# Interleaved key and query transposes, and a planner term for small TensorE jobs, in an attention and two-MoE kernel

## The chip, the cores and the metric

One core of a Trainium2 chip runs the whole kernel in one launch. The metric is the device time of an execution in microseconds; a lower one is better.

## The reference, cut to what matters

Three parts follow each other: chunked attention with memory keys, a dense feed-forward layer, and a top-1 mixture of eight experts. The change touches the first alone.

```python
def _attn_ref(q, k, v, mem_k, mem_v):      # q, k, v: 4 x 8 heads x 768 x 64; 8 memory keys
    chunk, left_ctx, right_ctx = (32, 16, 8)
    ...
    for c in range(nc):
        ...
        k_full = np.concatenate([mem_k, k_ctx], axis=2)
        scores = scale * np.matmul(q_c, k_full.transpose(0, 1, 3, 2))
        a = np.exp(scores - np.max(scores, axis=-1, keepdims=True))
        a = a / (np.sum(a, axis=-1, keepdims=True) + 1e-09)
        out[:, :, c_start:c_end] = np.matmul(a, v_full)

def reference(**kwargs):
    ...
    x = _moe_ref(x=x, **moe_kwargs)         # h = x @ w_in; (h * tanh(softplus(h))) @ w_out
    return _moe2_ref(x=x, **moe2_kwargs)    # one expert of eight for each token
```

## The kernel before, in words

Attention goes by 48 blocks of 64 queries, all eight heads of a block at once. Blocks 0 to 17 are made by `blocks`, 18 to 47 by `chunks`; the diff changes `chunks` alone. An even block brings 96 new keys (8 of memory, 24 of context, 64 others) and the odd block behind it 64 more; the pair shares one tile of transposed keys, `kT`. For each block there are these jobs: load of queries and keys (`load_qk`, lines 545 to 557), the transposes `T` (lines 581 to 592: four of queries, line 586, and four of keys, line 588, each of two heads), copies `qT` and `kT` out of PSUM, the scores `S` (line 616, 32 small matmuls in parts of the array), maximum, exponential and normalisation on VectorE and ScalarE, the transposes `PT` of the probabilities (line 646), the values `V` (line 662, 32 small matmuls in parts), and their split into a high and a low part, which feed the dense layer.

The dense layer works in steps `H` (line 748, twelve matmuls of 384 columns) and `Y` (line 794, nine of 512). Its output tiles are transposed (`yT`, line 854) and multiplied with the expert embedding (`yL`, line 886). After all that come the routing tables and the experts, 13 units beside those that a device-side branch adds.

In the trace a TensorE instruction's shape stands before its operands: 64*128 is 64 rows of the array by 128 columns. A transpose multiplies a 64x128 piece of queries, as weights, with a 64x64 identity; a piece of an even block's keys has 96 rows and a 96x96 identity.

The order of all work on all engines is made when the program is built, by `Plan.order` (lines 136 to 195). It keeps a clock for each engine; each job has a time on each engine that can do it, a rank, the jobs it comes after, and the buffers that it gets and uses. Of the jobs that are ready within 34 ns of an engine's next free moment it takes the one with the lowest key (line 166), and for TensorE the first part of that key is whether the last job was "tiled" (`V`, and `S` without a mask) and this one isn't. `between` (lines 98 to 106) adds a fixed time where TensorE goes from dense to small jobs and back. Three PSUM buffers with the tag `a` serve the small jobs: `T` of a block gets two, `V` in `chunks` two, `S`, `PT`, `yT` and `yL` one each. The chip then runs each engine's jobs in that order, each waiting for what it needs.

Of the kernel before, what the change touches and what calls it, by code (L numbers as in the profile page):

```python
# [9 lines left out]
F32 = mybir.dt.float32  # L10
# [9 lines left out]
B, H, S, D = 4, 8, 768, 64  # L20
NMEM = 8
CHUNK, LEFT, RIGHT = 32, 16, 8
QB = 64
CTX = QB + LEFT + RIGHT
NK = CTX + NMEM
# [66 lines left out]
TICK, WARM = 10240 / 3, 3600  # L92
SHARE = dict(T=0.62, S=0.76)
LATENCY, START, SLACK = 2000.0, 1100.0, 34.0
DENSE = {"mm_h", "mm_y", "H", "Y"}


def between(a, b):

    if a in DENSE:  # L100
        return 92 if b in ("T", "S", "yL") else 0
    if b in DENSE:
        return 0 if a is None else 20 if a in ("PT", "yT", "xT", "hT") else 90
    return 93 if a in ("PT", "yT") and b in ("T", "S") else 0
# [6 lines left out]
class Plan:  # L111
# [5 lines left out]
    def job(self, key, fn, on, rank, after=(), get=(), use=(), lat=130, tiled=False):  # L117
        uses = list(use) + [h for _, h in get]
        for h in uses:
            self.users.setdefault(h, []).append(key)  # L120
        for _, h in get:
            self.getter[h] = key
        self.jobs[key] = dict(fn=fn, on=on, rank=rank, after=list(after), get=list(get), use=list(use), lat=lat, tiled=tiled,
                              need=[(tag, sum(t == tag for t, _ in get)) for tag in dict(get)])
# [11 lines left out]
    def order(self):  # L136
        end, on, free, todo, waits, tiled, last, cols, port = {}, {}, {}, {}, {}, False, None, {}, 0.0
        shared = lambda k, e: e == "Pool" and k[0] not in ("gather", "scatter", "issue", "experts") or e == "DVE" and k[0] in PORT
        held = {tag: [None] * n for tag, n in self.bufs.items()}
        for k, j in self.jobs.items():  # L140
            j["deps"] = set(j["after"]) | {self.getter[h] for h in j["use"] if self.getter[h] != k}
            todo[k] = len(j["deps"])
            for d in j["deps"]:
                waits.setdefault(d, []).append(k)
        self.log = []
        ready = {k: START for k, n in todo.items() if n == 0}
        while ready:
            cand = {}
            for k, r in ready.items():
                j = self.jobs[k]  # L150
                for tag, n in j["need"]:
                    rel = sorted(self.release(h, end) for h in held[tag])
                    r = max(r, rel[n - 1])
                if r < np.inf:
                    begin = lambda e: max(r, free.get(e, 0.0), port if shared(k, e) else 0.0)
                    t, e, d = min((begin(e) + d + (d if shared(k, e) else 0), e, d) for e, d in j["on"].items())
                    t = begin(e)

                    cand.setdefault(e, []).append((t, r if e == "Q" else j["rank"], k, d))
            if not cand:  # L160
                raise RuntimeError(f"no room for any of {list(ready)}")
            picks = []
            for e, c in cand.items():
                t = max(min(x[0] for x in c), free.get(e, 0.0))

                picks.append((e, *min((x for x in c if x[0] <= t + SLACK), key=lambda x: (e == "PE" and tiled > self.jobs[x[2]]["tiled"], x[1], x[0]))))
            e, t, rank, k, d = min(picks, key=lambda x: (x[1], x[0]))
            j = self.jobs[k]
            del ready[k]
            for tag, h in j["get"]:  # L170
                x = min(held[tag], key=lambda h: self.release(h, end))
                held[tag][held[tag].index(x)] = h
            if e == "PE":

                t0 = free.get(e, FILL0)
                while ("mm_h", 0) not in end and t0 + FILL < t:
                    self.log.append((t0, t0, e, None))
                    t0 = self.stream(cols, t0, FILL, 1)
                t = max(t, t0)
                t += between(last, k[0])  # L180
                last, tiled = k[0], j["tiled"]
                d = self.stream(cols, t, d, SHARE.get(k[0], 1)) - t
            free[e] = t + d
            if shared(k, e):
                port = t + d
            end[k] = t + d + j["lat"]
            on[k] = e
            self.log.append((t, t + d, e, k))
            for w in waits.get(k, ()):
                todo[w] -= 1  # L190
                if todo[w] == 0:
                    chain = "PE" in self.jobs[w]["on"]
                    ready[w] = max(end[x] - (130 if chain and on[x] == "PE" else 0) for x in self.jobs[w]["deps"])
        assert len(end) == len(self.jobs)
        return [(k, e) for _, _, e, k in self.log]
# [20 lines left out]
def attn_moe_moe_kernel(ctx, tc, q, k, v, mem_k, mem_v, w_in, w_out, emb, tau, w1, w2, cst, out, ydbg=None):  # L216
    nc = tc.nc
# [5 lines left out]
    ident = cf[:, 0:128]  # L223
# [10 lines left out]
    att = pa.enter_context(tc.tile_pool(name="att", bufs=1))  # L234
# [8 lines left out]
    def psa(shape, name):  # L243
        return ps_a.tile(shape, F32, tag="a", name=name)
# [3 lines left out]
    job, A, V_, G, E = plan.job, "Activation", "DVE", "Pool", "PE"  # L248
    engs = {A: nc.scalar, V_: nc.vector, G: nc.gpsimd}
    xt, yp = {}, {}  # L250
    tl = {}
# [278 lines left out]
    def chunks(u):  # L530
        b, i = divmod(u, NQB)
        j, o = divmod(u, SPB)
        R = lambda x: x + (1.4 * u - 17.5 if u < (LEAVE + 1) * SPB else 2 * o + 32 if j == LEAVE + 1 else 8 * u / 3 - 20.4)
        J = H // 2
        odd, pair = u % 2, u // 2
        w = QB * i - LEFT
        edge = 0 if i == 0 else 1 if i == NQB - 1 else None
        new = QB if odd else NMEM + PREV + QB
# [4 lines left out]

        def load_qk(e):
            qn = tl["qn", u] = att.tile([QB, H, D], F32, tag="qn", bufs=1, name="qn")
            kn = tl["kn", u] = att.tile([NK, H, D], F32, tag="kn", bufs=1, name="kn")
            get = lambda n, x, lo, hi: nc.sync.dma_start(out=kn[n:n + hi - lo], in_=x[b, :, lo:hi, :].rearrange("h p d -> p h d"))
            nc.sync.dma_start(out=qn, in_=q[b, :, i * QB:(i + 1) * QB, :].rearrange("h p d -> p h d"))
            if not odd:
                get(0, mem_k, 0, NMEM)  # L550
            lo, hi = w + (PREV if odd else 0), w + PREV + QB
            n = 0 if odd else NMEM
            if lo < 0:
                get(n, k, 0, -lo)
            if hi > NQB * QB:
                get(n + NQB * QB - lo, k, 0, hi - NQB * QB)
            get(n + max(-lo, 0), k, max(lo, 0), min(hi, NQB * QB))
# [23 lines left out]
        def T(e):  # L581
            p1 = psa([128, J, QB], "p_qT")
            p2 = psa([128, J, new], "p_kT")
            a, c = tl["qn", u], tl["kn", u]
            for n in range(J):
                nc.tensor.transpose(p1[:, n, :], a[:, 2 * n:2 * n + 2, :].rearrange("p h d -> p (h d)"), ident[:QB, :QB])
            for n in range(J):
                nc.tensor.transpose(p2[:, n, :], c[0:new, 2 * n:2 * n + 2, :].rearrange("p h d -> p (h d)"), ident[:new, :new])
            tl["T", u] = p1, p2
            tl["qT", u] = att.tile([128, J, QB], F32, tag="qT", name="qT")  # L590
            if not odd:
                tl["kT", pair] = att.tile([128, J, 5 * GR - NMEM], F32, tag="kT", name="kT")
# [78 lines left out]
        def x_lo(e):  # L671
            for a in range(2):
# [7 lines left out]
        t1, t2 = ("a", u, 1), ("a", u, 2)  # L680
        pss, pr, mxh, sm = ("pS", u), ("pr", u), ("mx", u), ("sm", u)
        kt, xb = ("kT", pair), [("X", u), ("X2", u)]
        job(("T", u), T, {E: 560 if odd else 630}, rank=R(0), after=[("qk", u)], use=[(t, u) for t in ("qn", "kn")] + ([kt] if odd else []),
            get=[("a", t1), ("a", t2), ("qT", ("qT", u))] + ([] if odd else [("kT", kt)]))
        job(("qT", u), qT, {A: 264, V_: 330}, rank=R(1), after=[("T", u)], use=[t1, ("qT", u)])
        job(("kT", u), kT, {A: 264, V_: 330} if odd else {A: 371 + 210, V_: 465 + 200}, rank=R(1), after=[("T", u)], use=[t2, kt])
# [22 lines left out]
             + [(j, f) for j in reversed(range(LEAVE)) for f in range(HALF, KFF)]  # L709
             + [(j, f) for j in range(LEAVE + 1, NBLK) for f in range(KFF)])  # L710
    at = {x: s for s, x in enumerate(order)}
    done = [TPB * j + t for j in sorted(range(NBLK), key=lambda j: at[j, KFF - 1]) for t in range(TPB)]
    y_p = dram.tile([LEAVE * BLK, DM], F32, name="y_p")
# [885 lines left out]
    for u in range(NSUB):  # L1599
        (blocks if u < BY_CHUNK else chunks)(u)  # L1600
# [7 lines left out]
    for kind, n in TURNS:  # L1608
        c = FIRST + 2 * n
# [50 lines left out]
```

## Time and profile before

| | us |
|---|---|
| median of three runs | 1073.29 |
| lowest, highest | 1073.01, 1078.38 |
| the profiled execution | 1077.64 |
| its span, first to last instruction | 1075.9 |
| TensorE busy | 1044.6 (97%) |
| VectorE busy | 751.5 (70%) |
| ScalarE busy | 692.2 (64%) |
| GpSimd busy | 168.0 (16%) |

The profiled execution is one of its own, not one of the three runs. Busy time of TensorE counts overlapping matmuls once; each matmul's record is longer than its share of the engine, since the next begins before it has ended. So the time that a group of matmuls takes is read from starts, not from durations.

### The profile page before, as it was taken

Reading aid. Unit: us, or ns where it says so; the run is one execution under the profiler, and the core shown is the slowest. Engines: PE = TensorE matmul, PEld = TensorE weight load, DVE = VectorE, ACT = ScalarE, POOL = GpSimd, SP = SyncE. Lnnn points to the kernel's source line nnn. Section 1 sums busy time; section 2 is a strip of 40 time slices with the busy share of each in tenths; the row PEclk is TensorE's granted clock in tenths of the full one; section 3 lists DMA queues with packets and bytes.
Section 4 is the critical chain, followed back from the end, with each engine's and each line's share of the span. In section 5 each row is a group of like instructions: output and inputs, shape, how many; then the busy total and the mean of one; then the engine's idle time right before and its main releaser. Section 6 shows DMA issues by size and latency. Waiting matters only on the chain. (4 is left out here: it accounts for less than half of the span.)

```text
span 1075.9 us, 22578 instructions
## 1 busy us (share of the span) xinstructions
PE 1044.6 (97%) x8404; PEld 912.3 (85%) x8404; DVE 751.5 (70%) x1607; ACT 692.2 (64%) x1617; POOL 168.0 (16%) x109
## 2 busy tenths in 40 slices
PE   8899999999999999999999999998999999999996
PEld 6678888998888888888888889888899888988995
DVE  5999996556756566556556556886978657777851
ACT  4888887777757777777777777855633444443441
POOL 0000100000000000000000000010135645655552
PEclk9899999999999999999999999998999999999998
DMA  7966540032331112112112100019459877568200
GB/s 192 258 195 183 160 128 23 1 101 62 97 80 40 41 41 60 40 43 61 41 40 70 28 17 31 1 27 378 173 188 399 292 227 250 170 216 268 88 30 22
DMA packets 164019, 128.09 MB, mean 119 GB/s; under 512 B 106229, under 2 KB 135285, under 8 KB 163647
## 3 DMA queue, kind: packets, MB, share of 16 engines
q1 hardware_dynamic: 159439, 111.63, 34.4%
q0 software_dynamic: 4464, 14.95, 3.9%
q8 instruction: 69, 1.13, 0.4%
q14 instruction: 47, 0.39, 0.1%
HBM read 119.19 MB, written 16.52 MB: 126 GB/s over the span
## 5 line engine op out<-in xcount | busy, mean ns | idle before, releaser
L748 PE MATMUL p_h<-xt,win_h 128*128 128x384 f32 x1024 | 273.3, 348 | 1.7 <-DVE rn L777 1.5
L748 PEld LDWEIGHTS p_h<-xt,win_h 128*128 128x128 f32 x1024 | 183.0, 190 | 9.4 <-DVE rn L777 3.2
L748 PE MATMUL p_h<-xt,win_l 128*128 128x384 f32 x512 | 174.2, 340 | 0.0
L767 DVE SCALAR_TENSOR_TENSOR m<-sq,rn 128x384 f32<-128x384 f32 x128 | 71.8, 561 | 123.1 <-ACT rn L256 122.4
L794 PE MATMUL p_y<-wout_h,gh 128*128 128x512 f32 x384 | 155.9, 406 | 0.5 <-DVE gh L266 0.5
L266 ACT CAST ehi<-eraw 128x1024 fp32r<-128x1024 f32 x89 | 92.8, 1048 | 98.5 <-PE p_y L1496 51.5
L1378 DVE TENSOR_TENSOR elo<-eraw,ehi 128x1024 fp32r<-128x1024 f32 x89 | 125.6, 1419 | 42.6 <-ACT ehi L266 35.8
L794 PE MATMUL p_y<-wout_h,gl 128*128 128x512 f32 x384 | 151.8, 395 | 0.0
L794 PE MATMUL p_y<-wout_l,gh 128*128 128x512 f32 x384 | 151.4, 394 | 0.0
L1496 PE MATMUL p_y<-ehi,hh 128*128 128x512 f32 x432 | 142.1, 398 | 1.0 <-DVE hh L1465 1.0
L1406 PE MATMUL p_h<-xs,ehi 128*128 128x256 f32 x704 | 129.5, 285 | 0.0
L752 ACT ACTIVATE sq<-p_h 128x384 f32<-128x384 f32 x128 | 62.4, 488 | 78.4 <-PE p_h L748 78.0
L1406 PEld LDWEIGHTS p_h<-xs,ehi 128*128 128x128 f32 x704 | 111.0, 191 | 1.6 <-DVE xs L1359 0.4
L1378 POOL TENSOR_TENSOR elo<-eraw,ehi 128x1024 fp32r<-128x1024 f32 x39 | 96.9, 2484 | 79.8 <-ACT ehi L266 51.7
L1406 PE MATMUL p_h<-xs,elo 128*128 128x256 f32 x352 | 100.4, 285 | 0.0
L771 ACT ACTIVATE m<-m,few 128x384 f32<-128x384 f32 x128 | 79.1, 618 | 32.1 <-DVE m L767 31.2
L1300 POOL DMA_INDIRECT vn<-y_d,gi x27 | 27.6, 1023 | 453.3 <-DVE si L1247 402.7
L1496 PEld LDWEIGHTS p_y<-ehi,hh 128*128 128x128 f32 x432 | 81.1, 188 | 19.6 <-DVE hh L1465 2.3
L748 PEld LDWEIGHTS p_h<-xt,win_l 128*128 128x128 f32 x512 | 97.0, 190 | 0.0
L794 PEld LDWEIGHTS p_y<-wout_h,gl 128*128 128x128 f32 x384 | 72.2, 188 | 17.7 <-DVE gl L785 0.4
L1496 PE MATMUL p_y<-elo,hh 128*128 128x512 f32 x216 | 85.3, 395 | 0.0
L774 DVE SCALAR_TENSOR_TENSOR rn<-m,rn 128x384 f32<-128x384 f32 x128 | 70.8, 553 | 20.4 <-ACT m L771 19.1
(285 smaller groups left out, 1872.3 us busy)
## 6 DMA issues: line engine op xcount, KB each, us to landing
eraw<-in_moe_w_dram SPq DMA_DIRECT2D x128, 512.0 KB
raw<-in_moe_w_in_dram SPq DMA_DIRECT2D x16, 512.0 KB
raw<-in_moe_w_out_dram SPq DMA_DIRECT2D x16, 512.0 KB
y_d<-ysb SPq DMA_DIRECT2D x24, 256.0 KB
qn<-in_q_dram SPq DMA_DIRECT2D x43, 128.0 KB
vn<-in_v_dram SPq DMA_DIRECT2D x114, 32.0 KB
vn<-in_v_dram SPq DMA_DIRECT2D x122, 24.0 KB
kn<-in_k_dram SPq DMA_DIRECT2D x22, 128.0 KB
```

The costliest lines, as they stand in the source:

```text
L266: (nc.scalar.copy if e == A else nc.vector.tensor_copy)(out, src)
L748: nc.tensor.matmul(p, w, xt[j][:, a, kk, :], start=(n == 0), stop=(n == len(ops) - 1))
L752: nc.scalar.activation(t, tl["h", s], AF.Tanh, scale=0.5)
L767: nc.vector.scalar_tensor_tensor(t, tl["sq", s], 4.0, tl["rn", s], ALU.add, ALU.mult)
L771: nc.scalar.activation(t, t, AF.Square, bias=c15)
L774: nc.vector.scalar_tensor_tensor(tl["rn", s], tl["m", s], 0.75, tl["rn", s], ALU.add, ALU.mult)
L794: nc.tensor.matmul(yp[yh][t], x[:, c], w[g][:, o, :], start=(first and n == 0), stop=(final and n == 2))
L1300: nc.gpsimd.indirect_dma_start(out=tl["xg", u, a], out_offset=None, in_=y_d[0:T1 * 128, :] if g == 1 else y_d[:, :], in_offset=bass.Indire ...
L1378: engs[e].tensor_sub(tl["elo", j], raw[b, second, c], tl["ehi", j].bitcast(F32))
L1406: nc.tensor.matmul(p[:, o, :], w[:, kk, s], v[:, kk, :], start=(kk == 0 and m == 0), stop=(kk == KDM - 1 and m == 2))
L1496: nc.tensor.matmul(tl["yy", u][a], v[:, kk, s], w[:, k, :], start=(kk == 0 and m == 0), stop=(kk == KEF - 1 and m == 2))
```

## The change

Three things. In `chunks`, the key tile becomes 128 partitions tall, and an odd block's 64 new keys are loaded to its partitions 64 to 127, where they were on 0 to 63; an even block's 96 stay on 0 to 95. The transposes of queries and of keys, which were two loops of four, become one loop that issues one of each in turn, for odd and even blocks alike; the odd keys' use the lower right part of the identity. And the planner gets a time of 330 for an odd block's `T` in place of 560, and a new reason to put a job late on TensorE: the last job was one of `T`, `S`, `V`, `yL`, and this one isn't.

```diff
+SMALL = {"T", "S", "V", "yL"}
...
-                picks.append((e, *min((x for x in c if x[0] <= t + SLACK), key=lambda x: (e == "PE" and tiled > self.jobs[x[2]]["tiled"], x[1], x[0]))))
+                picks.append((e, *min((x for x in c if x[0] <= t + SLACK), key=lambda x: (e == "PE" and (tiled > self.jobs[x[2]]["tiled"] or last in SMALL and x[2][0] not in SMALL), x[1], x[0]))))
...
-            kn = tl["kn", u] = att.tile([NK, H, D], F32, tag="kn", bufs=1, name="kn")
+            kn = tl["kn", u] = att.tile([128, H, D], F32, tag="kn", bufs=1, name="kn")
...
-            n = 0 if odd else NMEM
+            n = QB if odd else NMEM
...
             a, c = tl["qn", u], tl["kn", u]
+
+            r = slice(QB, QB + new) if odd else slice(0, new)
             for n in range(J):
                 nc.tensor.transpose(p1[:, n, :], a[:, 2 * n:2 * n + 2, :].rearrange("p h d -> p (h d)"), ident[:QB, :QB])
-            for n in range(J):
-                nc.tensor.transpose(p2[:, n, :], c[0:new, 2 * n:2 * n + 2, :].rearrange("p h d -> p (h d)"), ident[:new, :new])
+                nc.tensor.transpose(p2[:, n, :], c[r, 2 * n:2 * n + 2, :].rearrange("p h d -> p (h d)"), ident[r, r])
...
-        job(("T", u), T, {E: 560 if odd else 630}, rank=R(0), after=[("qk", u)], use=[(t, u) for t in ("qn", "kn")] + ([kt] if odd else []),
+        job(("T", u), T, {E: 330 if odd else 630}, rank=R(0), after=[("qk", u)], use=[(t, u) for t in ("qn", "kn")] + ([kt] if odd else []),
```

## Rows read from the trace of the kernel before

**Rows 1.** The page: busy time of each engine, and TensorE's granted clock in 40 slices.
```profile
PE 1044.6 (97%) x8404; PEld 912.3 (85%) x8404; DVE 751.5 (70%) x1607; ACT 692.2 (64%) x1617; POOL 168.0 (16%) x109
...
PEclk9899999999999999999999999998999999999998
```

**Rows 2.** TensorE's waits, those for the keys' copies: us in total, times, longest us.
```profile
PE p_S L616 <- ACT kT L266: 3.8, 2, 2.1
```

**Rows 3.** Windows: stretch, length, busy us (instructions) by engine; then granted clock, DMA share, GB/s.
```profile
150.00:158.00 8.00, 6.43 (x37) 5.37 (x35) 8.00 (x17) 7.61 (x18) 0.00 (x0) 1.00 0.44 117
...
230.00:620.00 390.00, 388.49 (x3805) 333.84 (x3804) 244.80 (x593) 288.80 (x794) 0.60 (x1) 1.00 0.22 54
320.50:324.00 3.50, 3.25 (x55) 2.29 (x52) 2.90 (x6) 3.18 (x8) 0.00 (x0) 1.00 0.54 170
```

**Rows 4.** Groups of TensorE by form: count, busy us, mean ns of one, idle before.
```profile
L586 PE MATMUL p_qT<-cf,qn 64*128 64x64 f32 x120 | 13.9, 237 | 0.0
...
L588 PE MATMUL p_kT<-cf,kn 96*128 96x96 f32 x60 | 8.2, 260 | 0.0
L588 PE MATMUL p_kT<-cf,kn 64*128 64x64 f32 x60 | 6.3, 228 | 0.0
...
L886 PE MATMUL p_lg<-embT,yb 128*128 128x24 bf16 x84 | 5.5, 176 | 0.0
```

**Rows 5.** Timeline of TensorE, an odd block's transposes: start, length of the run, count.
```profile
301.24 0.46 PE L586 MATMUL p_qT<-cf,qn 64*128 64x64 f32 x4
301.53 0.41 PE L588 MATMUL p_kT<-cf,kn 64*128 64x64 f32 x4
301.87 0.62 PE L748 MATMUL p_h<-xt,win_h 128*128 128x384 f32 x2
```

**Rows 6.** Timeline of TensorE, values and scores, the same columns.
```profile
304.18 0.67 PE L662 MATMUL p_X<-pT,vn 64*64 64x32 f32 x32
304.78 0.65 PE L616 MATMUL p_S<-kT,qT 64*32 64x64 f32 x32
```

**Rows 7.** Timeline of TensorE, an even block; last three rows from narrower windows inside it.
```profile
309.95 0.46 PE L586 MATMUL p_qT<-cf,qn 64*128 64x64 f32 x4
...
310.67 0.47 PE L794 MATMUL p_y<-wout_h,gh 128*128 128x512 f32 x1
...
310.19 0.22 PE L586 MATMUL p_qT<-cf,qn 64*128 64x64 f32 x1
310.34 0.30 PE L588 MATMUL p_kT<-cf,kn 96*128 96x96 f32 x1
...
310.48 0.41 PE L588 MATMUL p_kT<-cf,kn 96*128 96x96 f32 x3
```

**Rows 8.** Timeline of TensorE, a block of `blocks` with 56 keys.
```profile
73.52 0.46 PE L410 MATMUL p_qT<-cf,qn 64*128 64x64 f32 x4
73.81 0.41 PE L412 MATMUL p_kT<-cf,kn 56*128 56x56 f32 x4
```

**Rows 9.** Timeline of TensorE, blocks 18 and 19, with idle time and its releaser.
```profile
158.08 0.65 PE L616 MATMUL p_S<-kT,qT 64*32 64x64 f32 x32 [1.65 <-ACT kT L266]
...
165.41 0.65 PE L616 MATMUL p_S<-kT,qT 64*32 64x64 f32 x32 [2.12 <-ACT kT L266]
165.99 0.62 PE L748 MATMUL p_h<-xt,win_h 128*128 128x384 f32 x2
...
169.47 0.63 PE L794 MATMUL p_y<-wout_h,gh 128*128 128x512 f32 x1
```

**Rows 10.** Timeline of TensorE, routing logits among dense matmuls.
```profile
593.48 0.40 PE L794 MATMUL p_y<-wout_h,gl 128*128 128x512 f32 x1
593.72 0.46 PE L886 MATMUL p_lg<-embT,yb 128*128 128x24 bf16 x12
594.03 0.48 PE L794 MATMUL p_y<-wout_h,gh 128*128 128x512 f32 x1
594.35 0.39 PE L794 MATMUL p_y<-wout_l,gh 128*128 128x512 f32 x1
```

## The prediction

> **What bounds the kernel now.** I read the page first: TensorE is busy for 1044.6 us, 97% of the span, at the full granted clock but for a few slices; VectorE has 70%, ScalarE 64% [rows 1]. A busy share alone proves nothing, so next come TensorE's waits: of its 1075.9 - 1044.6 = 31.3 idle us the one line of any size inside the changed blocks is 3.8 us, two waits of the scores for a copy of the keys [rows 2]. Then the stages: from 230 to 620 us, where most of the changed blocks are, TensorE is busy for 388.5 of 390 us, VectorE for 245, ScalarE for 289 [rows 3]. There a nanosecond on TensorE is a nanosecond of the end. Only around blocks 18 and 19 is it otherwise: from 150 to 158 us TensorE is busy for 6.4 of 8 us, VectorE for 8.0 and ScalarE for 7.6 [rows 3].
>
> The durations come from one execution of 1077.64 us (1.74 us of it outside its span of 1075.9); the median of the three runs is 1073.29. I sum differences and add them to the median.
>
> **Part 1, odd blocks.** There are 120 transposes of queries and 120 of keys, the keys half with 96 rows and half with 64: 30 blocks, 15 even (96 new keys) and 15 odd (64) [rows 4]. In an odd block the queries' four take 0.46 us from the first start to the last end; with 0.22 for one, their starts span 0.24. The keys' four take 0.41, so their starts span 0.19, or 0.063 a step [rows 5]. From the first start at 301.24 to the last at 301.53 + 0.19 = 301.72 it is 0.48 us. After the change a key's transpose uses rows 64 to 127 of the array and follows a query's on rows 0 to 63. What two such parts do together is not in these rows; the nearest are the value matmuls, which go round four parts of the array: 32 of them in 0.67 us, so (0.67 - 0.22)/31 = 0.0145 a step, and 0.058 a round, loads included [rows 6]. Four parts go round in what one transpose takes now, so I take it that two do: the eight starts span 0.24 + 0.01 = 0.25. That saves 0.23 a block; at the worst the 128-column loads go one after another and nothing is saved.
>
> **Part 2, even blocks.** The diff puts the same loop round both kinds of block, and an even block's 96 keys can't stand beside its queries: both need rows 0 to 63. What the new order does there is to alternate between two shapes, 64x128 and 96x128. The price of a change of shape is in every even block now, once: the last query transpose starts at 310.19, the first key one at 310.34, or 0.15 where a step in the shape is 0.063, so 0.09 us of waiting. The next key transpose starts at 310.48, 0.14 later, where the steps after it are (0.41 - 0.246)/2 = 0.08: another 0.06, a load that nothing hides [rows 7]. After a change to the queries' shape it is 0.24 - 0.19 = 0.05 [rows 5]. It is the shape and not the other tile: a block with 56 keys, which fits the queries' shape, goes on to them 0.29 us after its first start [rows 8], one with 96 after 0.39 [rows 7]. And it is there between packed shapes: scores follow values at 304.78, 0.15 after the last value's start at 304.18 + 0.45 [rows 6].
>
> An even block now has one such change inside; afterwards seven. Six more: three to the keys' shape at 0.09 + 0.06, three to the queries' at 0.09 + 0.05, together 0.87 us, so 0.72 (309.95 to 310.67 [rows 7]) becomes 1.59. From both sides: nothing, if the changes cost nothing when only one transpose is in flight; 0.54, if the loads are hidden and the waits alone remain. I take 0.87, since every such row so far has both.
>
> Of the 15 pairs I count 14. The first stands before 166 us, where the scores of both its blocks wait for ScalarE's copies, 1.65 and 2.12 us [rows 9]; its longer and its shorter transposes are covered by these waits.
>
> Even: 14 x 0.87 = 12.2 us more. Odd: 14 x 0.23 = 3.2 less.
>
> **Part 3, what is late next.** The queries' copy can start only when the seventh transpose is done, not the fourth, but its reader, the score matmuls, comes at 304.78 where the transposes began at 301.24 [rows 5, 6], with dense matmuls between, so nobody waits. The number and size of the loads stay, on SP's queue too; odd keys land on partitions 64 to 127. The key tile's wait moves from the fifth to the second transpose; TensorE's list of waits has none for a transpose of that tile, and the line of any size in those blocks is the scores' [rows 2].
>
> **Part 4, the planner.** The new term makes a difference only after a small job that is not marked tiled: after values and unmasked scores the old term already marks everything untiled as late, and one more true reason changes nothing. After T it finds little to take: T holds two of the three PSUM buffers, values want two, and scores need T's own copies. What remains is the routing logits, 84 / 4 = 21 row tiles [rows 4]. Next to T they save one return to the dense matmuls: 594.03 to 594.35 is 0.32 where 593.48 to 593.72, a step of the same size, is 0.24, so 0.08 [rows 10]. At most 21 x 0.08 = 1.7 us, and about half already have a small neighbour; I take 0.5 less, with ends 0 and 1.7. The planner's shorter time for odd T shifts its clock and so the order from there on; I count that as noise (rival C).
>
> **Sum.** 12.2 - 3.2 - 0.5 = 8.5 us more: 1077.6 + 8.5 = 1086.1 for the profiled execution, 1073.3 + 8.5 = 1081.8 against the median. I forecast **1081.8 us**, slower by 0.8%; about 0.5%, or 5.4 us, is what a measurement of this kernel can tell from no change.
>
> **Rivals.**
>
> A, not slower: the alternation in even blocks is nearly free. Then 1073.3 - 3.7 = 1069.6. It decides where a change of shape costs under 3.7 / (14 x 6) = 0.044 us. For it: no row shows two changes one transpose apart. Against: each change in the rows costs three times that [rows 6, 7]. Chance 0.14; a third of it passes 0.5%.
>
> B, slower still: the stretched transposes let the granted clock fall. The price of a fall: the twelve dense matmuls from 165.99 to 169.47 took 3.48 us at half clock, those from 301.87 to 304.18 took 2.31 [rows 5, 6, 9], so 1.2 a fall; five falls give 1088. Against: from 320.5 to 324.0 us TensorE ran transposes and scores alone, 3.25 of 3.5 us, and the granted clock was 1.00 [rows 3]. Chance 0.06. The Trainium skill, page "TensorE: Matmul & The Clock Gate", Part 4, says that transposes do not count as TensorE activity in the way that matmuls do; by that rule every even block's 1.59 us would count as idle and B would be the likely case. The stretch at 320.5 us, mostly transposes, speaks against so much of it here.
>
> C, the new order decides: the stalls of 156 to 170 us (1.65 + 2.12 idle, and 1.2 at half clock as in B) are 5.0 us in all [rows 5, 6, 9]. A new order can lose them, 1076.8, or find as many elsewhere, 1086.8. For it: the planner picks from ready lists, so one time changed changes what follows. Against: 390 us of the changed stretch have 1.5 us idle, with nothing to win [rows 3]. Chance 0.12, half each way.
>
> D, the odd blocks don't go side by side: the loads take turns, 1081.8 + 3.2 = 1085.0. Chance 0.06, because the values' rounds say otherwise [rows 6].
>
> **How the numbers follow.** The forecast has 0.62; its own range is 1077 to 1085 (13 to 15 even blocks, the planner's ends, and some scatter of the order). Slower by over 0.5% (1078.7 and above): 0.57 of the forecast, B, half of C, D: 0.75. Within: 0.05, two thirds of A, half of C: 0.20. Faster: the rest of A, 0.05. The range takes in the forecast, D, C and half of A: 1069 to 1089.
>
> **What would show it.** In the new trace an even block's transposes should take about 1.6 us from the first to the next dense matmul, with key and query starts 0.2 apart, and an odd one's about 0.40 instead of 0.63, in pairs of starts some 0.01 apart. TensorE's idle time should stay near 31 us and the clock at 1.00 from 230 to 620 us. I am wrong if even blocks stay near 0.72 us (A), if the clock falls in that stretch (B), or if the transposes do as said and the stalls before 170 us or after 690 us move by more than 4 us (C).

## The result, and the profile after

The changed kernel takes 1079.51 us (median of 18 runs, 1075.58 to 1083.79); the kernel before, on the same chips, 1073.15 (18 runs, 1070.46 to 1078.38). The ratio is 1.0055, with a 95% interval from 1.0041 to 1.0068: slower by a half per cent. The forecast was 1081.8.

The profiled execution of the changed kernel took 1076.99 us, near the lower end of its runs, and that of before 1077.64, near the upper end of its own. So the two spans say nothing of the difference; what stands inside them does. The page of the changed kernel answers to [rows 1]:

```profile
span 1075.1 us, 22543 instructions
PE 1046.6 (97%) x8404; PEld 909.0 (85%) x8404; DVE 753.2 (70%) x1622; ACT 691.2 (64%) x1603; POOL 164.8 (15%) x108
...
PEclk9899999999999999999999999999999999999998
```

TensorE's waits in the changed kernel (us in total, times, longest) answer to [rows 2]:

```profile
PE p_yT L856 <- DVE yt L868: 2.0, 2, 1.0
...
PE p_yT L856 <- ACT kT L267: 0.9, 1, 0.9
PE p_PT L648 <- DVE yt L868: 0.8, 1, 0.8
PE p_yT L856 <- ACT pT L267: 0.8, 1, 0.8
```

The line for the scores that waited for the keys' copies, 3.8 us before, is not in the new list, and output transposes (`yT`) wait instead. The windows of the changed kernel, columns as in [rows 3]:

```profile
150.00:158.00 8.00, 7.52 (x37) 6.38 (x37) 8.00 (x17) 7.07 (x16) 0.00 (x0) 1.00 0.32 107
158.00:162.00 4.00, 4.00 (x21) 3.26 (x19) 4.00 (x9) 3.19 (x7) 0.00 (x0) 1.00 0.38 123
162.00:166.00 4.00, 4.00 (x22) 3.42 (x23) 3.48 (x9) 3.02 (x8) 0.00 (x0) 1.00 0.24 54
166.00:170.00 4.00, 4.00 (x22) 3.63 (x21) 3.73 (x11) 3.72 (x10) 0.00 (x0) 1.00 0.05 11
...
230.00:620.00 390.00, 384.97 (x3722) 325.14 (x3721) 238.87 (x583) 284.05 (x778) 0.60 (x1) 1.00 0.21 52
```

The same three short windows of the kernel before:

```profile
158.00:162.00 4.00, 3.82 (x44) 3.40 (x44) 4.00 (x9) 3.95 (x10) 0.00 (x0) 0.73 0.35 102
162.00:166.00 4.00, 1.88 (x42) 1.43 (x41) 3.33 (x10) 3.10 (x10) 0.00 (x0) 0.84 0.26 60
166.00:170.00 4.00, 4.00 (x19) 3.91 (x15) 3.71 (x20) 3.37 (x18) 0.00 (x0) 0.58 0.27 87
```

The hole before 170 us has closed, and the granted clock stays at 1.00, where it was 0.58 to 0.84. From 230 to 620 us TensorE is idle for 5.0 us, before for 1.5: 3.7 us of it stand before output transposes. What the even blocks' transposes lose between one start and the next is not idle time in this view, because each matmul's record reaches over the next one's start. Here is one even block and one odd block in the timeline of TensorE (start, length, count), to be held against [rows 5, 7]:

```profile
306.36 0.27 PE L589 MATMUL p_qT<-cf,qn 64*128 64x64 f32 x1
306.56 0.30 PE L590 MATMUL p_kT<-cf,kn 96*128 96x96 f32 x1
306.79 0.27 PE L589 MATMUL p_qT<-cf,qn 64*128 64x64 f32 x1
307.00 0.30 PE L590 MATMUL p_kT<-cf,kn 96*128 96x96 f32 x1
...
307.66 0.27 PE L589 MATMUL p_qT<-cf,qn 64*128 64x64 f32 x1
307.87 0.30 PE L590 MATMUL p_kT<-cf,kn 96*128 96x96 f32 x1
307.95 0.48 PE L796 MATMUL p_y<-wout_h,gh 128*128 128x512 f32 x1
...
318.12 0.27 PE L589 MATMUL p_qT<-cf,qn 64*128 64x64 f32 x1
318.13 0.27 PE L590 MATMUL p_kT<-cf,kn 64*128 64x64 f32 x1
318.23 0.22 PE L589 MATMUL p_qT<-cf,qn 64*128 64x64 f32 x1
318.24 0.22 PE L590 MATMUL p_kT<-cf,kn 64*128 64x64 f32 x1
...
318.36 0.22 PE L589 MATMUL p_qT<-cf,qn 64*128 64x64 f32 x1
318.36 0.22 PE L590 MATMUL p_kT<-cf,kn 64*128 64x64 f32 x1
```

The even block takes 307.95 - 306.36 = 1.59 us where one took 0.72; each start is 0.20 to 0.23 behind the last. The median over all 15 is 1.588 against 0.718: 1.585 to 1.590 in eleven blocks, 1.64 in the four where another small job comes next. In the odd block the starts come in pairs, and span 0.24 us in place of 0.48; from the first transpose to the next work the median of the 15 is 0.391 us against 0.635.

### The profile page after: what moved, and what is told of

It is laid out like the page before. It is cut to its first block, busy times and chain, and to the rows that moved or that the text cites. A ratio compares the mean times of both kernels' runs of the same rounds, so it can differ in the third digit from the quotient of the medians.

```text
span 1075.1 us, 22543 instructions
## 1 busy us (share of the span) xinstructions
PE 1046.6 (97%) x8404; PEld 909.0 (85%) x8404; DVE 753.2 (70%) x1622; ACT 691.2 (64%) x1603; POOL 164.8 (15%) x108
## 5 line engine op out<-in xcount | busy, mean ns | idle before, releaser
L750 PEld LDWEIGHTS p_h<-xt,win_h 128*128 128x128 f32 x1024 | 182.0, 189 | 8.9 <-DVE rn L779 2.6
L1380 DVE TENSOR_TENSOR elo<-eraw,ehi 128x1024 fp32r<-128x1024 f32 x89 | 123.3, 1394 | 41.5 <-ACT ehi L267 41.2
```

The lines of the kernel that those rows point to most:

```text
L750: nc.tensor.matmul(p, w, xt[j][:, a, kk, :], start=(n == 0), stop=(n == len(ops) - 1))
L1380: engs[e].tensor_sub(tl["elo", j], raw[b, second, c], tl["ehi", j].bitcast(F32))
```

## The experiments

The theory: the changes of shape in even blocks cost 0.87 us each block, odd blocks give 0.24 back, and the planner's two edits make up the rest. The rivals: the new order is the loss; or taking turns costs by itself, whatever the shapes.

Each ratio is to the kernel before on the same chip, over five rounds. The last three columns are starts of dense steps `H` (runs of twelve matmuls of 384 columns), counted in each profiled timeline; between the 25th and the 105th lie the transposes of 14 even and of 13 or 14 odd blocks.

| kernel | median us | ratio (95%) | 25th H | 105th H | 128th H |
|---|---|---|---|---|---|
| before (profiled) | | | 187.0 | 607.6 | 714.4 |
| changed | 1079.51 | 1.0055 (1.0041 to 1.0068) | 181.0 | 614.5 | 720.2 |
| odd_only | 1067.33 | 0.9931 (0.9907 to 0.9955) | 180.7 | 601.9 | 707.6 |
| t_old_order | 1085.04 | 1.0097 (1.0068 to 1.0125) | 185.8 | 616.9 | 723.4 |
| odd_only_old_order | 1073.19 | 0.9989 (0.9970 to 1.0008) | 184.8 | 604.0 | 710.8 |
| plan_only | 1072.28 | 0.9976 (0.9958 to 0.9995) | 181.5 | 605.0 | 710.9 |
| q96_mixed | 1065.04 | 0.9900 (0.9873 to 0.9928) | 181.2 | 599.5 | 705.2 |
| two_two | 1071.01 | 0.9957 (0.9941 to 0.9974) | 180.2 | 605.4 | 711.1 |
| small_only | 1068.76 | 0.9932 (0.9908 to 0.9957) | 182.0 | 602.8 | 709.5 |
| t330_only | 1076.90 | 1.0010 (0.9992 to 1.0028) | 189.2 | 611.6 | 718.0 |
| pair_late_33 | 1069.34 | 0.9956 (0.9934 to 0.9978) | 182.0 | 603.2 | 710.0 |
| q96_560 | 1063.07 | 0.9872 (0.9839 to 0.9904) | 181.9 | 598.1 | 704.6 |
| odd_560 | 1064.48 | 0.9896 (0.9867 to 0.9925) | 180.2 | 599.2 | 705.9 |
| even_told | 1080.06 | 1.0047 (1.0027 to 1.0067) | 182.9 | 615.5 | 721.3 |

**odd_only.** Even blocks go back to two loops of four.

```diff
             for n in range(J):
                 nc.tensor.transpose(p1[:, n, :], ...)
-                nc.tensor.transpose(p2[:, n, :], ...)
+                if odd:
+                    nc.tensor.transpose(p2[:, n, :], ...)
+            for n in range(0 if odd else J):
+                nc.tensor.transpose(p2[:, n, :], ...)
```

> The changed kernel with one thing taken back: even blocks do their four query transposes and then their four key transposes, as before; the order of all jobs is that of the changed kernel. If the shape changes in even blocks are the loss (0.87 us in each of 15), 1079.5 - 13.0 = 1066.5 us, 0.6% under the kernel before, and an even block's transposes go from 1.59 back to 0.72 us. If the new order of jobs is the loss, the time stays near 1079.5.

Measured: 1067.33 us, and the 105th H step comes at 601.9 in place of 614.5, 12.6 us earlier with the same order of jobs. An even block is back at its old pace (timeline of TensorE):

```profile
303.19 0.40 PE L799 MATMUL p_y<-wout_h,gl 128*128 128x512 f32 x1
303.52 0.46 PE L589 MATMUL p_qT<-cf,qn 64*128 64x64 f32 x4
303.91 0.55 PE L593 MATMUL p_kT<-cf,kn 96*128 96x96 f32 x4
304.24 0.48 PE L799 MATMUL p_y<-wout_h,gh 128*128 128x512 f32 x1
```

That is 304.24 - 303.52 = 0.72 us. The even blocks' turns are more than the whole loss: without them the rest of the change is faster than before.

**t_old_order, odd_only_old_order, plan_only.** The other halves: the changed transposes, or those of `odd_only`, under the planner of before (the edit below, and line 166 as it was); and the planner's two edits with the transposes of before.

```diff
-SMALL = {"T", "S", "V", "yL"}
...
-        job(("T", u), T, {E: 330 if odd else 630}, ...
+        job(("T", u), T, {E: 560 if odd else 630}, ...
```

> The changed transposes alone, odd and even, with the planner of before, so that the order of all jobs is that of the kernel before. If the transposes are the loss: 13.0 more in even blocks and 15 x 0.24 = 3.7 less in odd ones, 1073.2 + 9.3 = 1082.5, or 1081.7 if the pair of blocks 18 and 19 is covered by its waits. If the order is the loss: 1073.

> Side by side in odd blocks alone, with the planner of before. If an odd block's 0.24 us are worth their time at the end: 1073.2 - 3.5 = 1069.7. If something behind the transposes takes it back: 1073.

> The planner's part of the change alone (the term for small jobs, and 330 for an odd block's transposes), with the transposes of before. If the transposes are the loss, the planner's part is what is left of it: 1079.5 - 9.3 = 1070.2. If the order is the loss: 1079.5 or more. The stalls between 156 and 170 us should be gone, as in the changed kernel, and some waits of output transposes between 230 and 620 us be there.

Measured: the transposes alone cost 0.97% (forecast 9.3 us, which is 0.87%), the planner's edits alone win 0.24%, and the order as the loss has fallen. The odd blocks alone came out at 0.9989, where 3.5 us would be 0.9967; the interval, which reaches 0.9970, just misses it. How much of an odd block's 0.244 us reaches the end stays open. With one order of jobs, `plan_only` against `odd_only`, 14 odd blocks' transposes save 14 x 0.244 = 3.4 us between the 25th and the 105th H step, and the stretch gets shorter by 423.5 - 421.2 = 2.3; two more pairs with one order each, `small_only` against `odd_560` and the kernel before against `odd_only_old_order`, give 1.8 (of 3.4) and 1.4 (of 3.2, for 13 blocks). By the ratios the three pairs differ by 0.45%, 0.36% and 0.11%, where 3.7 us would be 0.34%. The traces show one way to lose a part: the job behind some odd block's transposes now comes before what it needs. TensorE's window from 230 to 620 us, columns as in [rows 3], in `small_only`, `plan_only` and `odd_only`:

```profile
230.00:620.00 390.00, 387.80 (x3832) 334.10 (x3831) 245.24 (x606) 287.90 (x789) 0.61 (x1) 1.00 0.22 55
230.00:620.00 390.00, 385.90 (x3830) 331.76 (x3829) 243.51 (x600) 290.04 (x797) 0.60 (x1) 1.00 0.21 53
230.00:620.00 390.00, 384.95 (x3841) 330.46 (x3840) 244.77 (x602) 291.17 (x799) 0.61 (x1) 1.00 0.22 53
```

From `plan_only` to `odd_only` the idle time grows from 4.1 to 5.0 us. In the changed kernel the output transposes behind the odd block at 318 us wait like that, 0.90 us where `plan_only` has 0.2 (timeline of TensorE):

```profile
318.65 0.44 PE L648 MATMUL p_PT<-cf,pr 128*128 128x128 f32 x2
319.99 1.09 PE L856 MATMUL p_yT<-cf,ysb 128*128 128x128 f32 x8 [0.90 <-ACT kT L267]
```

**q96_mixed.** The even blocks' queries get 96 rows, so that both kinds of transpose have one shape; the turns stay, and the copy out of PSUM takes the 64 columns that are needed.

```diff
-            qn = tl["qn", u] = att.tile([QB, H, D], F32, tag="qn", bufs=1, name="qn")
+            nq = QB if odd else NK
+            qn = tl["qn", u] = att.tile([nq, H, D], F32, tag="qn", bufs=1, name="qn")
...
-            nc.sync.dma_start(out=qn, in_=q[b, :, i * QB:(i + 1) * QB, :].rearrange("h p d -> p h d"))
+            nc.sync.dma_start(out=qn, in_=q[b, :, i * QB:i * QB + nq, :].rearrange("h p d -> p h d"))
...
-                nc.tensor.transpose(p1[:, n, :], a[:, 2 * n:2 * n + 2, :].rearrange("p h d -> p (h d)"), ident[:QB, :QB])
+                nc.tensor.transpose(p1[:, n, :], a[:, 2 * n:2 * n + 2, :].rearrange("p h d -> p (h d)"), ident[:nq, :nq])
```

> The changed kernel, but an even block's query tile is loaded with 96 rows (the 64 queries and the first 32 of the next block, which nobody reads), so that its query transposes have the key transposes' 96x128 shape; they still take turns. If it is the change of shape that costs, the turns are now free: no change inside and none on the way in, an even block's transposes near 0.70 us instead of 1.59, and 15 x 1.0 = 15 us less than the changed kernel, about 1064 us. If taking turns between two outputs costs by itself, it stays near 1.59 us and 1079.

The timeline of TensorE, from the last dense matmul to the next:

```profile
303.02 0.40 PE L798 MATMUL p_y<-wout_h,gl 128*128 128x512 f32 x1
303.25 0.25 PE L591 MATMUL p_qT<-cf,qn 96*128 96x96 f32 x1
303.34 0.24 PE L592 MATMUL p_kT<-cf,kn 96*128 96x96 f32 x1
303.42 0.24 PE L591 MATMUL p_qT<-cf,qn 96*128 96x96 f32 x1
...
303.83 0.25 PE L592 MATMUL p_kT<-cf,kn 96*128 96x96 f32 x1
303.86 0.48 PE L798 MATMUL p_y<-wout_h,gh 128*128 128x512 f32 x1
```

Taking turns is free: a start every 0.08 us, 0.61 for all eight where I expected 0.70, and the first comes 0.23 after the dense matmul before it, which is a dense matmul's own step; with 64 rows it is 0.33 (303.52 - 303.19 in `odd_only`). The 105th H step is 15.0 us earlier than in the changed kernel, as expected. So it is the shape that costs, on the way in from the dense matmuls too, and rival "turns" has fallen. Between dense matmuls and transposes of 96 rows there is no price on entry, with 64 rows there is.

**two_two.** Two and two in even blocks: three changes of shape in place of seven.

```diff
-            for n in range(J):
-                nc.tensor.transpose(p1[:, n, :], ...)
-                nc.tensor.transpose(p2[:, n, :], ...)
+            w = 1 if odd else 2
+            for m in range(0, J, w):
+                for n in range(m, m + w):
+                    nc.tensor.transpose(p1[:, n, :], ...)
+                for n in range(m, m + w):
+                    nc.tensor.transpose(p2[:, n, :], ...)
```

> The changed kernel, with two query transposes, then two key transposes, twice, in even blocks: three changes of shape in place of seven. If each change has its own price of 0.145 us, 15 x 4 x 0.145 = 8.7 us less than the changed kernel, 1070.8 us, and 1.01 us from the first transpose to the next dense matmul. If the price is only there when one transpose stands alone, or doesn't grow with the count, the 1.01 is another number: 0.72, or 1.59.

The timeline of TensorE:

```profile
303.83 0.33 PE L591 MATMUL p_qT<-cf,qn 64*128 64x64 f32 x2
304.10 0.38 PE L593 MATMUL p_kT<-cf,kn 96*128 96x96 f32 x2
304.41 0.33 PE L591 MATMUL p_qT<-cf,qn 64*128 64x64 f32 x2
304.68 0.38 PE L593 MATMUL p_kT<-cf,kn 96*128 96x96 f32 x2
304.84 0.48 PE L799 MATMUL p_y<-wout_h,gh 128*128 128x512 f32 x1
```

304.84 - 303.83 = 1.01 us, to the hundredth what was expected, and 1071.01 us against 1070.8. With one, three and seven changes inside, the block takes 0.72, 1.01 and 1.59 us: 0.145 for each, whatever stands between them.

**small_only, t330_only.** The planner's two edits apart, each on the kernel before. The first keeps this edit alone, the second the other:

```diff
+SMALL = {"T", "S", "V", "yL"}
...
-... key=lambda x: (e == "PE" and tiled > self.jobs[x[2]]["tiled"], x[1], x[0])
+... key=lambda x: (e == "PE" and (tiled > self.jobs[x[2]]["tiled"] or last in SMALL and x[2][0] not in SMALL), x[1], x[0])
```

```diff
-        job(("T", u), T, {E: 560 if odd else 630}, ...
+        job(("T", u), T, {E: 330 if odd else 630}, ...
```

> The kernel before with the planner's term for small jobs alone. If it is this term that moved the first pair of blocks past the stall between 156 and 170 us, that stall is gone here, and the time is that of the planner's part in whole, 0.9976 of before or a little more.

> The kernel before with the planner's 330 in place of 560 for an odd block's transposes alone, the transposes as before. If the term for small jobs made the order's gain, the stall between 156 and 170 us is still here, and the time is within 0.2% of before. If the 330 made it, the time is 0.9976 of before.

The term alone wins 0.68%, where I had expected the 0.24% of both together or a little more; from the 25th to the 105th H step `small_only` takes 420.8 us and `plan_only` 423.5. Most of that stands in the windows above as idle time, 2.2 us without the 330 and 4.1 with it: with the 330, output transposes wait 2.0 us for VectorE (`yt`) and 0.8 for ScalarE (`pT`), and in `small_only` for neither. The 330 alone wins nothing; on TensorE its order of jobs is that of before up to 415 us, and among TensorE's waits in its trace there is still the one that the term removes:

```profile
PE p_S L616 <- ACT kT L266: 3.9, 2, 2.3
```

On TensorE the order with the term first differs from before at block 16. There the values of block 15 follow the transposes at once (timeline of `small_only`); before, nine dense matmuls and a block's scores stood between:

```profile
110.98 0.46 PE L411 MATMUL p_qT<-cf,qn 64*128 64x64 f32 x4
111.37 0.55 PE L413 MATMUL p_kT<-cf,kn 96*128 96x96 f32 x4
111.85 0.69 PE L490 MATMUL p_X<-pT,vn 96*64 96x64 f32 x16
```

The merges themselves are few: up to the 128th H step TensorE goes from dense matmuls to small jobs 122 times before and 119 times in `small_only`, so 3 x 0.08 = 0.2 us by the forecast's price of one. Behind block 16 everything is arranged anew; in the changed kernel the transposes of blocks 18 and 19 begin at 161.7 and 221.6 us, where they began at 153.4 and 162.2.

**pair_late_33.** No term and no 330; the planner is only told to put the transposes of blocks 18 and 19 later.

```diff
-        job(("T", u), T, ..., rank=R(0), after=[("qk", u)], ...
+        job(("T", u), T, ..., rank=R(0), after=[("qk", u)] + ([("mm_h", {18: 19, 19: 33}[u])] if u < BY_CHUNK + 2 else []), ...
```

> The kernel before with its own transposes and planner; only the planner is told that the transposes of blocks 18 and 19 come after two later dense steps, so that the order around the stall between 156 and 170 us changes and little else. If the term for small jobs gained by moving this pair away from the stall, the stall is gone here too and the time is about 5 us under before, 0.995. If it gained in other ways, the time stays within 0.2% of before.

The windows of this kernel, columns as in [rows 3]:

```profile
150.00:158.00 8.00, 7.47 (x38) 6.51 (x37) 7.96 (x16) 7.61 (x17) 0.00 (x0) 1.00 0.34 95
158.00:162.00 4.00, 3.50 (x19) 2.94 (x18) 4.00 (x11) 3.16 (x8) 0.00 (x0) 1.00 0.39 142
162.00:166.00 4.00, 4.00 (x22) 3.64 (x21) 4.00 (x11) 2.80 (x6) 0.00 (x0) 1.00 0.02 4
166.00:170.00 4.00, 4.00 (x25) 3.26 (x24) 3.97 (x14) 3.84 (x8) 0.00 (x0) 1.00 0.00 1
```

The hole is gone, the granted clock does not fall, and the time is 0.9956 of before, with nothing merged. The 25th H step comes 5.0 us earlier than before, in `small_only` also 5.0; a part of that is work of blocks 18 and 19 that now comes behind it. At the 128th, when all blocks are done, it is 4.4 us here and 4.9 in `small_only`. So the term removed this stall, and the stall alone is worth 0.44% of the term's 0.68%: most of it, though the two intervals overlap. What the rest is stays open, and so does why the planner puts the pair later once block 15's values are done sooner.

**even_told.** The changed kernel with the true time of an even block's transposes in the plan.

```diff
-        job(("T", u), T, {E: 330 if odd else 630}, ...
+        job(("T", u), T, {E: 330 if odd else 1500}, ...
```

> The changed kernel, with the planner told 1500 in place of 630 for an even block's transposes. If the loss is TensorE's own time, telling the planner gives nothing back: 1.005 of before, within 0.3%. If the loss came from a plan made on a wrong time, it goes: 0.993, as without the turns in even blocks.

1.0047: nothing that the intervals can tell comes back. A plan that knows the time does not avoid the loss, which fits `odd_only`: it is TensorE's own time.

**q96_560, odd_560.** The parts that won, together: the term for small jobs, odd blocks side by side, the planner's old 560, with 96-row queries (an edit of `q96_mixed`) or without (of `odd_only`).

```diff
-        job(("T", u), T, {E: 330 if odd else 630}, ...
+        job(("T", u), T, {E: 560 if odd else 630}, ...
```

> The kernel with 96-row query tiles in even blocks, and the planner's 560 put back for odd ones, since the 330 took back part of what the term for small jobs gave (0.9976 with both, 0.9932 with the term alone). If that adds up, 0.990 - 0.0035 = 0.9865 of before or near it. If the 330 only moved things by chance of that order, 0.990 as without.

> Side by side in odd blocks alone, the term for small jobs, and the planner's 560. By the sum: 0.9932 for the term alone, less 3.6 us for the odd blocks, 0.990 of before. If the 330 matters nothing: 0.9931, as with it.

0.9872 and 0.9896, both as the sums say, though the intervals overlap those with 330 (0.9900 and 0.9931), so that the 560's own gain is not settled. `q96_560`, 1063.07 us, is faster than both the kernel before and the changed one.

## Why the prediction was right, and where not

**Odd blocks: right.** 0.39 us for 0.40 forecast. What the sum left out is that the 3.2 us (14 blocks) or 3.7 (15) need not all reach the end: of 3.2 to 3.4 us between the 25th and the 105th H step, 1.4 to 2.3 did, and 0.9 went into waits behind the shortened jobs in the one pair of traces above.

**Even blocks: right**, 1.59 for 1.59 in eleven of 15, 1.64 in the four with a small job behind them. The step that carried it was to trust the price of a change, wait and load, one transpose apart; that was rival A's question, and `two_two` and `q96_mixed` answer it. The Trainium skill, page "TensorEngine Tiling (Array Packing)", Key Properties, says that changing the tiling mode, and not just the tile, drains TensorE. This case's traces agree in what can be seen: 0.145 us for a change of shape, and 0.062 us a pair, nothing more, for going from one half of the rows to the other; whether the engine drains, their modelled ends do not show.

**14 of 15 pairs: wrong by one.** The cover that I named for blocks 18 and 19, the scores' waits for ScalarE, went with the new order: around block 18's transposes, at 161.7 us, TensorE is busy for 4.00 of 4 us. So all 15 paid, 13.0 us in place of 12.2.

**The planner: the step that failed.** I priced the term for small jobs at 0.5 us, with ends at 0 and 1.7, by counting what it could merge. The reasoning holds for `chunks`, where values want two buffers. It left out `blocks`, where they want one, and there the term finds values behind a block's transposes. And the gain is mostly not in a merge: the term won 0.68% alone, 0.44% of which is there when only one pair of blocks is moved past a stall, and 0.24% (0.05 to 0.42) beside the 330. With 3.7 x 2.3 / 3.4 = 2.5 us for the odd blocks, 13.0 - 2.5 - 2.6 (0.24% of 1073) = 7.9; by the other difference, from 1.0097 to 1.0055, the planner is worth 4.5, which leaves 6.0. The result was 6.4.

**Rival C came by half.** Its sign, stalls before 170 us that move by more than 4 us, is there: the 25th H step comes 6.0 us earlier, a part of it because block 19's work now stands behind that step. I had priced the stalls at 5.0, with one stretch of dense matmuls at the lower clock, and taken their loss for a toss of a coin. There were two such stretches (granted clock 0.73 from 158 to 162 us, 0.58 from 166 to 170; in neither were all twelve matmuls at half clock). The first is this, in the timeline of TensorE before:

```profile
158.83 0.63 PE L748 MATMUL p_h<-xt,win_h 128*128 128x384 f32 x2
...
162.18 0.69 PE L586 MATMUL p_qT<-cf,qn 64*128 64x64 f32 x4
```

Twelve dense matmuls take 3.35 us here, where 2.31 is the full pace [rows 5, 6]: 1.0 us that the sum left out. Against that gain stand the new order's own waits, 5.0 us of idle time from 230 to 620 us in place of 1.5, and the 15th pair; so the time is not C's 1076.8.

**Some of the nearness is luck.** The even blocks cost 0.8 us more than forecast and the odd ones saved about 0.7 less; the planner won 2.1 to 4.0 more. These misses have opposite signs, so the total is nearer to the result than the terms are, one by one.

**The clock: rival B did not come.** 14 even blocks of 1.59 us stand between 230 and 620 us with a granted clock of 1.00, the higher of the two levels. The Trainium skill, page "TensorE: Matmul & The Clock Gate", Part 4, says that transposes do not count as activity as matmuls do. No run here shows that: the transposes of the changed kernel cost no clock.

## What to carry to other kernels

Before small TensorE jobs are put in turns, look at their shapes in the trace: two of one shape on different halves of the rows ran beside each other here, but each change between 64 and 96 rows was paid, 0.145 us, and padding the smaller operand to the other's shape was cheaper than changing. An edit of a list scheduler can be worth more by what the new order does to a stall that the profile already shows than by what it merges; look for the stall first, and try to move it alone. And what a job saves on a full engine reaches the end only as far as the next job's inputs are ready.

## What the runs showed of the hardware that was not expected

- Two transposes on the two halves of the array start 0.002 to 0.009 us apart, most of them 0.003 or 0.004, and a pair takes 0.062 us, as long as one alone. The loads of 128 columns do not take turns: at 318.12 us the two of a pair start 0.003 us apart and take 0.135 us each.
- A transpose of 96 rows behind a dense matmul of 128 rows costs nothing on entry (0.23 us from start to start, the dense step); one of 64 rows comes 0.10 us later. 32 rows of data that nobody reads made an even block's eight transposes faster than before the change, 0.61 us against 0.72.
- The price of a change of shape is the same 0.145 us with two transposes or with one between the changes, and in all 15 blocks within 0.01 us, save where another job than a dense matmul comes next.
